# A decode step on one core: wq in plain transfers, weights of y kept in the array, and thirty-seven tiny transfers added

## The chip, the cores and the metric

The kernel runs on one core of a Trainium2 chip. A core has a matrix engine (TensorE, here PE, with its weight loads listed as PEld), a vector engine (DVE), a scalar engine (ACT), GpSimd (POOL), a sync engine (SP) that here only starts transfers, and 16 DMA engines that carry all transfers. The metric is the device time of one launch in microseconds (us), and lower is better.

## The reference

Two layers read the same normalised row and are added to the input row:

```python
x  = A_x                                  # 1 x 1 x 1024, bf16
xn = layernorm(x)
q  = (xn @ wq)                            # 32 heads of 128
k, v = last 4096 rows of the caches       # 4 kv heads, each for 8 query heads
o  = softmax(q @ k.T * 128**-0.5) @ v
A  = o.reshape(1, 1, 4096) @ wo
y  = layernorm(xn)
B  = gelu(y @ w1 + b1) @ w2 + b2          # 1024 -> 3584 -> 1024
out = x + A + B
```

One row goes in and one row comes out, so nearly all the work is reading weights and caches once: w1 and w2 of 7 MB each, wq and wo of 8 MB each, and the windows of K and V of 4 MB each.

## The kernel before, in words

The kernel is written engine by engine, with semaphores set by hand. Each engine runs its own list in order.

**Loads.** ACT starts three small loads: the row x into `XBR` (L165), b1 (L166), b2 (L167). SP starts everything large, in this order: W1 as one transfer (`load_rows`, L158), the first half of wq into `WA` (rows 0 to 3 of each partition, L158), the second half of wq in several pieces (below), two K transfers (L237), two V transfers (after the b1 products), W2 into the place of W1 (after the W1 products, semaphore count `C["h"]`), and wo into the place of wq, in pieces of 20, 10, 1 and 1 blocks (after the q products, `C["q"]`, L158). At the end it stores the row (L549).

**The second half of wq before.** Partition p holds rows 8p to 8p+7 of wq, and the second half is rows 4 to 7 of each. It is loaded in two transfers, one for the even partitions (L229) and one for the odd (L230). The odd one leaves out the last 1024 columns of row 7. These 64 pieces of 2 KB come in four transfers of 16 pieces (L233) into `WX`, a tile of 48 partitions that lies in `Pb`. Because those pieces then lie in other partitions, the product over them needs its own weights: `XPR` (x gathered by GpSimd, L183), two small products (L266), `XEZ` (L286), a copy of the weights of row 7 with the odd partitions set to zero (`EVEN`, `XNZ7`, L288 and L292), and four more products at the end of q (L354).

**Order of work.** The statistics of x and of xn (twice a short chain PE, DVE, ACT) are made while W1 is on its way. Then PE does y @ w1 (L324, 56 products, for 8 rows of `YTb` times 7 stretches of 512 columns), q (L345, 64 products, and L354), turns K (L405), scores (L431), softmax on DVE and ACT, P @ V (L510), W2 (L494) and wo (L494). Between the wo pieces stand five products of no use (L543). ACT copies the result (L547) and SP stores it.

Of the kernel before, what the change touches and what calls it, by code (L numbers as in the profile page):

```python
# [5 lines left out]
ALU = mybir.AluOpType  # L6
ACTF = mybir.ActivationFunctionType
AX = mybir.AxisListType
# [11 lines left out]
KC = D // 128  # L20
NQ = HQ * DH
WQ_CHUNKS = [4, 4]
W1_CHUNKS = [8]
W2_CHUNKS = [28]
WO_CHUNKS = [20, 10, 1, 1]
KEEP_BUSY = [[512] * 5, [], [], []]
NPAIR = HKV // 2
PB = 2 * NBLK
CUT = 1024
B1W = 256  # L30
B1N = F // B1W
XS = 2
XROWS = 48
OUTSIDE = -1e30
PAD = 32

# [13 lines left out]
def bass_parallel_sum__sliding_block_cached__mixer_channel_mlp__decode_kernel(  # L50
# [18 lines left out]
    pe, dve, act, pool, sp = nc.tensor, nc.vector, nc.scalar, nc.gpsimd, nc.sync  # L69

    def sems(name, n):
        return [nc.alloc_semaphore(f"{name}{i}") for i in range(n)]

    s_xrow, s_b1, s_b2, s_out = (nc.alloc_semaphore(n) for n in ("s_xrow", "s_b1", "s_b2", "s_out"))
    s_wq = sems("s_wq", len(WQ_CHUNKS))
    s_ex = nc.alloc_semaphore("s_ex")
    s_w1 = sems("s_w1", len(W1_CHUNKS))
    s_k = sems("s_k", NPAIR)
    s_v = sems("s_v", NPAIR)
# [4 lines left out]
    DVE = Track(nc, "S_DVE")  # L84
    ACT = Track(nc, "S_ACT")
    POOL = Track(nc, "S_POOL")

    def sb(name, shape, d):
        return nc.alloc_sbuf_tensor(name, shape, d)

    f32, bf16 = dt.float32, dt.bfloat16
    identb = sb("identb", [128, 128], bf16)
    identf = sb("identf", [128, 128], f32)
# [5 lines left out]
    oneb = sb("oneb", [128, 1], bf16)  # L99
    XBR = sb("XBR", [1, 2 * D], bf16)  # L100
    XT16 = sb("XT16", [128, 16], f32)
    msx = sb("msx", [128, 8], f32)
    XNT = sb("XNT", [128, 8], f32)
    XNTb = sb("XNTb", [128, 8], bf16)
    XNZ = sb("XNZ", [128, KC * 15], bf16)
    EVEN = sb("EVEN", [128, 1], f32)
    XNZ7 = sb("XNZ7", [128, 15], bf16)
    XPR = sb("XPR", [1, XS * XROWS], bf16)
    XEZ = sb("XEZ", [XROWS, XS * 15], bf16)
    YT16 = sb("YT16", [128, 16], f32)  # L110
    msy = sb("msy", [128, 8], f32)
    EXPW = sb("EXPW", [128, 1], f32)
# [12 lines left out]
    Pb = sb("Pb", [128, PB * HQ], bf16)  # L125
# [9 lines left out]
    W1 = sb("W1", [128, KC * F], bf16)  # L135
    W2 = W1[:, 0:FC * D]
    WA = sb("WA", [128, KC * NQ], bf16)
    WX = Pb[0:XROWS, 0:XS * CUT]
    PS = nc.alloc_psum_tensor("PS", [128, 8 * 512], f32)
    PSb = PS[:, :].bitcast(bf16)  # L140

# [1 line left out]
    b2_row = B_b2.rearrange("(o n) -> o n", o=1)  # L143
    b1_row = B_b1.rearrange("(o n) -> o n", o=1)
    wq_p = A_wq.rearrange("(p r) n -> p r n", r=KC)
    wq_runs = A_wq.rearrange("(p r) n -> p (r n)", r=KC)
    wq_x = A_wq.rearrange("(s h r e k) n -> k s h e r n", s=XS, h=2, r=4, e=4)[2 * KC - 1]
    w1_p = B_w1.rearrange("(p r) n -> p r n", r=KC)
    w2_p = B_w2.rearrange("(p c) n -> p c n", c=FC)
    wo_p = A_wo.rearrange("(p j) n -> p j n", j=32)  # L150
    out_rows = out.rearrange("b s (a n) -> (b s a) n", a=4)

    C = {}

    def load_rows(dst, src, chunks, width, semaphores):
        c0 = 0
        for j, n in enumerate(chunks):
            sp.dma_start(  # L158
                dst[:, c0 * width:(c0 + n) * width].rearrange("p (c n) -> p c n", c=n),
                src[:, c0:c0 + n, :],  # L160
            ).then_inc(semaphores[j], 16)
            c0 += n
# [3 lines left out]
    act.dma_start(B1R, b1_row.rearrange("o (c n) -> o c n", c=B1N)).then_inc(s_b1, 16)  # L166
    act.dma_start(XBR[:, D:2 * D], b2_row).then_inc(s_b2, 16)  # L167

    POOL.mark(pool.memset(WA[:, KC * NQ - CUT:KC * NQ], 0.0))
    C["hole"] = POOL.mark(pool.memset(WX, 0.0))  # L170
    POOL.mark(pool.memset(XPR[:, :], 0.0))
    C["oneb"] = POOL.mark(pool.memset(oneb[:, :], 1.0))
    C["onesf"] = POOL.mark(pool.memset(onesf[:, :], 1.0))
    POOL.mark(pool.memset(identb[:, :], 0.0))
# [1 line left out]
    C["identb"] = POOL.mark(pool.affine_select(  # L176
        out=identb[:, :], in_=identb[:, :], pattern=[[-1, 128]], compare_op=ALU.not_equal,
        fill=1.0, base=0, channel_multiplier=1))
    pool.wait_ge(s_xrow, 16)
    for i in range(XS):  # L180
        at = i * 2 * 16 * 2 * KC
        dst = XPR[0:1, i * XROWS:(i + 1) * XROWS].rearrange("o (g m) -> o g m", g=3)[:, 0:3:2, :]
        C["xpr"] = POOL.mark(pool.tensor_copy(  # L183
            dst.rearrange("o h (e r) -> o h e r", e=4),
            XBR[0:1, at + 2 * KC - 1:at + 2 * 16 * 2 * KC:2 * KC].rearrange("o (h r e) -> o h e r", h=2, e=4)))
    POOL.mark(pool.memset(identf[:, :], 0.0))
    pool.wait_ge(POOL.sem, POOL.cnt)
    C["identf"] = POOL.mark(pool.affine_select(
        out=identf[:, :], in_=identf[:, :], pattern=[[-1, 128]], compare_op=ALU.not_equal,
        fill=1.0, base=0, channel_multiplier=1))  # L190
    POOL.mark(pool.memset(XNZ[:, :], 0.0))
    POOL.mark(pool.memset(XNZ7[:, :], 0.0))
    C["xnz"] = POOL.mark(pool.memset(XEZ[:, :], 0.0))
    POOL.mark(pool.memset(E4[:, :], 0.0))
    POOL.mark(pool.memset(GMASK[:, :], 1.0))
    pool.wait_ge(POOL.sem, POOL.cnt)
# [1 line left out]
        out=E4[:, :].rearrange("p (q m) -> p q m", q=4), in_=E4[:, :].rearrange("p (q m) -> p q m", q=4),  # L198
        pattern=[[1, 4], [-1, 128]], compare_op=ALU.not_equal, fill=1.0, base=0, channel_multiplier=4))
    POOL.mark(pool.affine_select(  # L200
        out=GMASK[:, :], in_=GMASK[:, :], pattern=[[-2 * REP, NPAIR]], compare_op=ALU.is_ge, fill=0.0,
# [10 lines left out]
    at = PAR[:, :].rearrange("k (m g) -> k m g", g=2)  # L212
# [7 lines left out]
    pool.wait_ge(POOL.sem, POOL.cnt)  # L220
    POOL.mark(pool.memset(OT[:, 32:32 + PAD], 0.0))
    C["consts"] = POOL.cnt


    load_rows(W1, w1_p, W1_CHUNKS, F, s_w1)
    load_rows(WA, wq_p, WQ_CHUNKS[:-1], NQ, s_wq)
    sp.wait_ge(POOL.sem, C["hole"])
    c0 = (KC - WQ_CHUNKS[-1]) * NQ
    sp.dma_start(WA[0:128:2, c0:KC * NQ], wq_runs[0:128:2, c0:KC * NQ]).then_inc(s_wq[-1], 16)  # L229
    sp.dma_start(WA[1:128:2, c0:KC * NQ - CUT], wq_runs[1:128:2, c0:KC * NQ - CUT]).then_inc(s_wq[-1], 16)  # L230
    for i in range(XS):
        for h in range(2):
            sp.dma_start(WX[32 * h:32 * h + 16, i * CUT:(i + 1) * CUT], wq_x[i, h, :, :, NQ - CUT:NQ]).then_inc(s_ex, 16)  # L233

    def load_cache(dst, cache, semaphores):
        for i in range(NPAIR):
# [23 lines left out]
    pe.wait_ge(s_xrow, 16)  # L260
    for r in range(KC):
        last = pe.matmul(xt[:, r:r + 1], lhsT=XBR[0:1, r:D:KC], rhs=oneb[0:1, :])
    xe = PS[0:XROWS, 7 * 512 + 24: 7 * 512 + 24 + XS]
    pe.wait_ge(POOL.sem, C["xpr"])
    for i in range(XS):
        last = pe.matmul(xe[:, i:i + 1], lhsT=XPR[0:1, i * XROWS:(i + 1) * XROWS], rhs=oneb[0:1, :])  # L266
    C["xt"] = PE.mark(last)
    dve.wait_ge(PE.sem, C["xt"])
    DVE.mark(dve.tensor_copy(XT16[:, 0:8], xt))
# [12 lines left out]
    dve.wait_ge(DVE.sem, DVE.cnt)  # L282
    DVE.mark(dve.tensor_scalar(out=XNT[:, :], in0=XT16[:, 0:8], scalar1=msx[:, 2:3], scalar2=msx[:, 7:8],
                               op0=ALU.subtract, op1=ALU.mult))
    dve.wait_ge(POOL.sem, C["xnz"])
    DVE.mark(dve.tensor_scalar(out=XEZ[:, 7:XS * 15:15], in0=xe, scalar1=msx[0:XROWS, 2:3], scalar2=msx[0:XROWS, 7:8],  # L286
                               op0=ALU.subtract, op1=ALU.mult))
    C["even"] = DVE.mark(dve.tensor_reduce(out=EVEN[:, 0:1], in_=identf[:, 0:128:2], axis=AX.X, op=ALU.add))  # L288
    dve.wait_ge(DVE.sem, DVE.cnt)
    C["xn"] = DVE.mark(dve.tensor_copy(XNTb[:, :], XNT[:, :]))  # L290
    pool.wait_ge(DVE.sem, C["xn"])
    C["xnz7"] = POOL.mark(pool.tensor_tensor(out=XNZ7[:, 7:8], in0=XNTb[:, KC - 1:KC], in1=EVEN[:, 0:1], op=ALU.mult))  # L292
    dve.wait_ge(DVE.sem, DVE.cnt)
    C["xnz_d"] = DVE.mark(dve.tensor_copy(XNZ[:, 7:KC * 15:15], XNTb[:, :]))
    DVE.mark(dve.tensor_copy(YT16[:, 0:8], XNTb[:, :]))
# [7 lines left out]
    C["std2"] = ACT.mark(act.activation(out=msy[:, 6:7], in_=msy[:, 5:6], func=ACTF.Sqrt))  # L303
    act.wait_ge(ACT.sem, ACT.cnt)
    ACT.mark(act.activation(out=EXPW[:, 0:1], in_=msy[:, 6:7], func=ACTF.Exp))
    dve.wait_ge(ACT.sem, C["std2"])
    DVE.mark(dve.reciprocal(out=msy[:, 7:8], in_=msy[:, 6:7]))
    dve.wait_ge(DVE.sem, DVE.cnt)
# [10 lines left out]
    k = 0  # L319
    for j, n in enumerate(W1_CHUNKS):  # L320
        pe.wait_ge(s_w1[j], 16)
        for _ in range(n):
            for t in range(7):
                last = pe.matmul(  # L324
                    PS[0:1, t * 512:(t + 1) * 512], lhsT=YTb[:, k:k + 1],
                    rhs=W1[:, k * F + t * 512: k * F + (t + 1) * 512],
                    start=False, stop=(k == KC - 1))
            k += 1
# [6 lines left out]
    pe.wait_ge(DVE.sem, C["d_sum"])  # L335
    k = 0
    for j, n in enumerate(WQ_CHUNKS):
        pe.wait_ge(s_wq[j], 16 if j < len(WQ_CHUNKS) - 1 else 32)
        for _ in range(n):
            for t in range(8):  # L340
                cut = k == KC - 1 and (t + 1) * 512 > NQ - CUT
                if cut:
                    pe.wait_ge(POOL.sem, C["xnz7"])
                z = XNZ7[:, 7 - t:15 - t] if cut else XNZ[:, 15 * k + 7 - t:15 * k + 15 - t]
                pe.matmul(  # L345
                    PS[0:8, 7 * 512:8 * 512], lhsT=z,
                    rhs=WA[:, k * NQ + t * 512: k * NQ + (t + 1) * 512],
                    start=(k == 0 and t == 0), stop=False)
            k += 1
    pe.wait_ge(s_ex, 32 * XS)  # L350
    for i in range(XS):
        for t in range((NQ - CUT) // 512, 8):
            at = i * CUT + t * 512 - (NQ - CUT)
            last = pe.matmul(  # L354
                PS[0:8, 7 * 512:8 * 512], lhsT=XEZ[:, 15 * i + 7 - t:15 * i + 15 - t], rhs=WX[:, at:at + 512],
                start=False, stop=(i == XS - 1 and t == 7))
    C["q"] = PE.mark(last)
    dve.wait_ge(PE.sem, C["q"])
    C["d_q8"] = DVE.mark(dve.tensor_copy(Q8[:, :], PS[0:8, 7 * 512:8 * 512]))  # L359
# [183 lines left out]
            pe.matmul(PS[0:32, 0:n], lhsT=OT[:, 0:32], rhs=WA[:, 0:n])  # L543
    C["fin"] = PE.mark(last)

    act.wait_ge(PE.sem, C["fin"])
    C["a_out"] = ACT.mark(act.activation(out=ORow[:, :], in_=PS[:, 6 * 512:6 * 512 + 256], func=ACTF.Copy))  # L547
    sp.wait_ge(ACT.sem, C["a_out"])
# [32 lines left out]
```

## Time and profile before

| | |
|---|---|
| time, median of 2 runs | 100.94 us (100.84 to 101.05) |
| profiled execution, span from first to last instruction | 99.4 us |
| PE, DVE, ACT, POOL busy | 69.6, 25.8, 12.8, 9.0 us |
| bytes moved, mean rate | 39.96 MB, 402 GB/s |
| main DMA queue (SP) | 1832 packets, 39.85 MB |
| W1 products (L324) | start 20.28, 14.43 us |
| q products (L345, L354) | end 49.49 us |
| last wo products (L494) | start 95.64, 1.61 us |

The profile lists one execution. The span is counted from the first instruction to the last, and the device time of a run holds some 1.5 us more than it (100.94 against 99.4). The row of DMA digits on the page gives the mean busy share of the 16 DMA engines in 40 slices of about 2.5 us. The list of waits names for each idle stretch what ended it. Beside these views the trace holds a record of every DMA packet: its queue, start, duration and size, but not its engine. Packets that follow each other on one engine can be chained, since one starts within a few nanoseconds of the end of the other.

### The profile page before, as it was taken

How to read it: one execution, taken by the hardware profiler on the slowest of the kernel's cores; microseconds unless marked ns; L12 is line 12 of the kernel's file. 1: busy time of each engine (PE TensorE's matmuls, PEld its weight loads, DVE VectorE, ACT ScalarE, POOL GpSimd, SP SyncE). 2: the span in 40 equal slices, each digit the busy share in tenths (PEclk: the TensorE clock that was granted, in tenths of full speed). 3: DMA queues.
4: the chain of work that ended last, by engine and by line, in shares of the span. 5: the costliest groups of instructions: out<-in, count | busy, mean ns of one | idle time of the engine just before them, and what ended most of it. 6: DMA issues, size and time to landing. Idle time of an engine off the chain costs nothing.

```text
span 99.4 us, 1681 instructions
## 1 busy us (share of the span) xinstructions
PE 69.6 (70%) x763; PEld 42.4 (43%) x763; DVE 25.8 (26%) x50; ACT 12.8 (13%) x15; POOL 9.0 (9%) x30
## 2 busy tenths in 40 slices
PE   0230860089999999999999999722799995009961
PEld 0220300023434343434399869510567894008740
DVE  0058500000000090000078921867790040000000
ACT  0500240000000050000065730005200000000001
POOL 7989100000000000000000000000000000000000
PEclk9999999999999999999999999555557999855799
DMA  9988889999999999999999999998999899699930
GB/s 347 392 372 369 370 369 485 465 422 422 422 422 422 409 402 403 441 429 442 429 429 422 429 534 416 468 485 369 392 485 425 346 445 528 287 404 437 405 143 1
DMA packets 1870, 39.96 MB, mean 402 GB/s; under 512 B 244, under 2 KB 262, under 8 KB 584
## 3 DMA queue, kind: packets, MB, share of 16 engines
q1 hardware_dynamic: 1832, 39.85, 94.1%
q8 instruction: 6, 0.10, 0.4%
q10 hardware_dynamic: 32, 0.01, 0.0%
HBM read 39.86 MB, written 0.00 MB: 401 GB/s over the span
## 4 chain that ended last, share of the span: by engine, by line
DMA 65%; PE 31%; ACT 0%; SPq 0%; issue 0%
DMA WA<-in_A_wo_dram 46%; DMA W<-in_B_w_dram 19%; PE PS L324 15%; PE PS L345 14%; PE PS L494 2%; PE PS L354 1%; ACT ORow L547 0%; SPq L158 0%
## 5 line engine op out<-in xcount | busy, mean ns | idle before, releaser
L324 PE MATMUL PS<-W,YTb 128*1 128x512 bf16 x56 | 14.4, 425 | 6.2 <-DMA W<-in_B_w_dram 6.2
L345 PE MATMUL PS<-WA,XNZ 128*8 128x512 bf16 x64 | 14.0, 379 | 0.0
L324 PEld LDWEIGHTS PS<-W,YTb 128*1 128x1 bf16 x56 | 5.1, 91 | 16.0 <-issue 10.3
L510 PE MATMUL PS<-KV,Pb 128*32 128x256 bf16 x64 | 10.0, 333 | 1.2 <-ACT Pb L471 1.2
L494 PE MATMUL PS<-WA,OT 128*32 128x256 bf16 x128 | 5.6, 345 | 7.1 <-DMA WA<-in_A_wo_dram 7.1
L345 PEld LDWEIGHTS PS<-WA,XNZ 128*8 128x8 bf16 x64 | 5.6, 88 | 8.2
L510 PEld LDWEIGHTS PS<-KV,Pb 128*32 128x32 bf16 x64 | 7.4, 118 | 3.9 <-ACT Pb L471 1.7
L494 PEld LDWEIGHTS PS<-WA,OT 128*32 128x32 bf16 x128 | 4.5, 123 | 8.4 <-issue 6.3
L333 DVE CAST ROW<-PS 1x2048 bf16<-1x2048 f32 x1 | 2.3, 2279 | 22.2 <-PE PS L324 22.2
L417 ACT ACTIVATE KV<-PS 128x1024 bf16<-128x1024 bf16 x6 | 5.8, 1021 | 16.1 <-PE PS L405 16.1
L405 PE MATMUL PS<-identb,KV 128*128 128x128 bf16 x128 | 7.5, 219 | 0.0
L405 PEld LDWEIGHTS PS<-identb,KV 128*128 128x128 bf16 x128 | 7.2, 98 | 0.5 <-issue 0.4
L412 DVE COPY KV<-PS 128x1024 bf16<-128x1024 bf16 x10 | 6.4, 686 | 1.1 <-PE PS L405 1.1
L331 ACT ACTIVATE ROW<-PS 1x1536 bf16<-1x1536 f32 x1 | 1.4, 1440 | 21.2 <-PE PS L324 21.2
L359 DVE CAST Q<-PS 8x512 bf16<-8x512 f32 x1 | 0.7, 678 | 12.5 <-PE PS L354 12.5
L475 DVE TENSOR_REDUCE SUMP<-Pb 128x32 f32<-128x2048 bf16 x1 | 3.6, 3566 | 1.2 <-ACT Pb L471 1.2
L547 ACT ACTIVATE ORow<-PS 128x256 bf16<-128x256 f32 x1 | 0.4, 384 | 27.0 <-PE PS L494 27.0
L299 PE MATMUL PS<-YT,onesf 128*128 128x16 f32 x2 | 0.6, 383 | 4.2 <-DVE YT L297 4.2
L431 PEld LDWEIGHTS PS<-QT,KV 128*128 128x128 bf16 x128 | 3.3, 96 | 0.4 <-issue 0.4
L494 PE MATMUL PS<-W,GT 128*32 128x256 bf16 x112 | 3.4, 273 | 0.0
L431 PE MATMUL PS<-QT,KV 128*128 128x16 bf16 x128 | 3.4, 169 | 0.0
L442 DVE TENSOR_REDUCE MXP<-PS 128x32 f32<-128x2048 f32 x1 | 2.3, 2292 | 3.9 <-PE PS L431 3.9
(104 smaller groups left out, 48.8 us busy)
## 6 DMA issues: line engine op xcount, KB each, us to landing
W<-in_B_w_dram SPq DMA_DIRECT2D x2, 7168.0 KB, 31.0
WA<-in_A_wo_dram SPq DMA_DIRECT2D x1, 5120.0 KB, 40.0
WA<-in_A_wq_dram SPq DMA_DIRECT2D x1, 4096.0 KB, 28.6
KV<-in_A_k_cache_dram SPq DMA_DIRECT2D x2, 2048.0 KB, 40.2
KV<-in_A_v_cache_dram SPq DMA_DIRECT2D x2, 2048.0 KB, 43.6
WA<-in_A_wo_dram SPq DMA_DIRECT2D x1, 2560.0 KB, 45.7
WA<-in_A_wq_dram SPq DMA_DIRECT2D x1, 2048.0 KB, 31.2
WA<-in_A_wq_dram SPq DMA_DIRECT2D x1, 1920.0 KB, 36.7
```

The lines of the kernel that those rows point to most:

```text
L324: last = pe.matmul(PS[0:1, t * 512:(t + 1) * 512], lhsT=YTb[:, k:k + 1], rhs=W1[:, k * F + t * 512: k * F + (t + 1) * 512], start=False, s ...
L331: C["a_hrow"] = ACT.mark(act.activation(out=Hrow[:, 0:1536], in_=PS[0:1, 0:1536], func=ACTF.Copy))
L333: C["d_hrow"] = DVE.mark(dve.tensor_copy(Hrow[:, 1536:F], PS[0:1, 1536:F]))
L345: pe.matmul(PS[0:8, 7 * 512:8 * 512], lhsT=z, rhs=WA[:, k * NQ + t * 512: k * NQ + (t + 1) * 512], start=(k == 0 and t == 0), stop=False)
L405: last = pe.matmul(PSb[:, o:o + 128], lhsT=KT[:, col + bb * 128: col + (bb + 1) * 128], rhs=identb[:, :], is_transpose=True)
L412: C["dkt"][u] = DVE.mark(dve.tensor_copy(KT[:, col + 1024 * s: col + 1024 * (s + 1)], PSb[:, bk * 1024:(bk + 1) * 1024]))
L417: C["akt"][u] = ACT.mark(act.activation(out=KT[:, col + 1024: col + 2048], in_=PSb[:, bk * 1024:(bk + 1) * 1024], func=ACTF.Copy))
L431: last = pe.matmul(PS[:, o:o + 2 * REP], lhsT=KT[:, (i * PB + b) * 128:(i * PB + b + 1) * 128], rhs=QT[:, i * 2 * REP:(i + 1) * 2 * REP], ...
L442: C["mxp"] = DVE.mark(dve.tensor_reduce(out=MXP[:, :], in_=PS[:, 0:2048].rearrange("p (b n) -> p n b", b=PB), axis=AX.X, op=ALU.max))
L475: C["sump"] = DVE.mark(dve.tensor_reduce(out=SUMP[:, :], in_=Pb[:, :].rearrange("p (b n) -> p n b", b=PB), axis=AX.X, op=ALU.add))
L494: ins = pe.matmul(acc(a), lhsT=vec[:, c:c + 32], rhs=weights[:, c * D + a * 256: c * D + (a + 1) * 256], start=False, stop=(c == stop_at))
L510: last = pe.matmul(PS[0:32, 4 * 512:4 * 512 + NPAIR * DH], lhsT=Pb[:, b * HQ:(b + 1) * HQ], rhs=V4[:, :, b, :], start=(b == 0), stop=(b == ...
```

## The change

- The second half of wq becomes a plain transfer of all 128 partitions, like the first. The four transfers of `WX`, and all that served them (`XPR`, `XEZ`, `EVEN`, `XNZ7`, two large and some small fills on GpSimd (L169 to L171, L192, L193), SP's wait for these fills, six products on PE), go away.
- In y @ w1 the weights, one row of `YTb`, are loaded by the first of the seven products of a row. The other six (`again`) are issued without a weight load.
- ACT starts 15 tiny loads (`marks`) after its second table load: the n-th reads n rows of 4n bytes of x. It starts the same 15 again after the gelu's exponent, and before its last copy waits for all of them.
- GpSimd starts seven tiny loads (`PROBES`) of 2 to 7 rows, two runs of 6 to 18 bytes in each row, after its constants. ACT waits for them before the second set.

```diff
+PROBES = [3, 5, 4, 6, 7, 2, 5]
...
+    def again(out, lhsT, rhs, start, stop):
+        return pe.add_instruction(mybir.InstMatmult(
+            name=nc.get_next_instruction_name(), engine=pe.engine, ins=[pe.lower_ap(rhs), pe.lower_ap(lhsT)], outs=[pe.lower_ap(out)],
+            start_tensor_calc=start, stop_tensor_calc=stop, ldweights=False, tile_size=(128, 32), tile_position=(0, 0)))
...
+    def marks():
+        for n in range(1, 16):
+            act.dma_start(MK[0:n, n * (n - 1):n * (n + 1)],
+                          A_x.rearrange("b s (k n) -> (b s k) n", n=64)[0:n, 0:2 * n]).then_inc(s_mark, 16)
...
+    for i, n in enumerate(PROBES):
+        pool.wait_ge(s_xrow, 16)
+        pool.dma_start(
+            MP[16 * i:16 * i + n, :].rearrange("p (a n) -> p a n", a=2)[:, :, 0:i + 3],
+            A_x.rearrange("b s (k a n) -> (b s k) a n", a=2, n=32)[0:n, :, 0:i + 3]).then_inc(s_probe, 16)
...
     load_rows(W1, w1_p, W1_CHUNKS, F, s_w1)
-    load_rows(WA, wq_p, WQ_CHUNKS[:-1], NQ, s_wq)
-    sp.wait_ge(POOL.sem, C["hole"])
-    c0 = (KC - WQ_CHUNKS[-1]) * NQ
-    sp.dma_start(WA[0:128:2, c0:KC * NQ], wq_runs[0:128:2, c0:KC * NQ]).then_inc(s_wq[-1], 16)
-    sp.dma_start(WA[1:128:2, c0:KC * NQ - CUT], wq_runs[1:128:2, c0:KC * NQ - CUT]).then_inc(s_wq[-1], 16)
-    for i in range(XS):
-        for h in range(2):
-            sp.dma_start(WX[32 * h:32 * h + 16, i * CUT:(i + 1) * CUT], wq_x[i, h, :, :, NQ - CUT:NQ]).then_inc(s_ex, 16)
+    load_rows(WA, wq_p, WQ_CHUNKS, NQ, s_wq)
...
     ACT.mark(act.activation(out=EXPW[:, 0:1], in_=msy[:, 6:7], func=ACTF.Exp))
+    marks()
...
             for t in range(7):
-                last = pe.matmul(
+                put = pe.matmul if t == 0 else again
+                last = put(
                     PS[0:1, t * 512:(t + 1) * 512], lhsT=YTb[:, k:k + 1],
...
+    act.wait_ge(s_probe, 16 * len(PROBES))
+    act.wait_ge(s_mark, 16 * 15)
+    marks()
+    act.wait_ge(s_mark, 2 * 16 * 15)
     act.wait_ge(PE.sem, C["fin"])
     C["a_out"] = ACT.mark(act.activation(out=ORow[:, :], in_=PS[:, 6 * 512:6 * 512 + 256], func=ACTF.Copy))
```

More of the change, by code (lines that the diff above doesn't have):

```diff
@@ L28 @@
 PB = 2 * NBLK
-CUT = 1024
 B1W = 256
 B1N = F // B1W
-XS = 2
-XROWS = 48
 OUTSIDE = -1e30
@@ L72, in sems @@
         return [nc.alloc_semaphore(f"{name}{i}") for i in range(n)]
+    s_mark = nc.alloc_semaphore("s_mark")
+    s_probe = nc.alloc_semaphore("s_probe")
     s_xrow, s_b1, s_b2, s_out = (nc.alloc_semaphore(n) for n in ("s_xrow", "s_b1", "s_b2", "s_out"))
     s_wq = sems("s_wq", len(WQ_CHUNKS))
-    s_ex = nc.alloc_semaphore("s_ex")
     s_w1 = sems("s_w1", len(W1_CHUNKS))
@@ L104, in bass_parallel_sum__sliding_block_cached__mixer_channel_mlp__decode_kernel @@
     XNTb = sb("XNTb", [128, 8], bf16)
+    MK = sb("MK", [128, 240], bf16)
+    MP = sb("MP", [128, 20], bf16)
     XNZ = sb("XNZ", [128, KC * 15], bf16)
[L106 to L109, printed above, removed]
     YT16 = sb("YT16", [128, 16], f32)
@@ L137, in bass_parallel_sum__sliding_block_cached__mixer_channel_mlp__decode_kernel @@
     WA = sb("WA", [128, KC * NQ], bf16)
-    WX = Pb[0:XROWS, 0:XS * CUT]
     PS = nc.alloc_psum_tensor("PS", [128, 8 * 512], f32)
@@ L145, in bass_parallel_sum__sliding_block_cached__mixer_channel_mlp__decode_kernel @@
     wq_p = A_wq.rearrange("(p r) n -> p r n", r=KC)
-    wq_runs = A_wq.rearrange("(p r) n -> p (r n)", r=KC)
-    wq_x = A_wq.rearrange("(s h r e k) n -> k s h e r n", s=XS, h=2, r=4, e=4)[2 * KC - 1]
     w1_p = B_w1.rearrange("(p r) n -> p r n", r=KC)
@@ L167, in bass_parallel_sum__sliding_block_cached__mixer_channel_mlp__decode_kernel @@
     act.dma_start(XBR[:, D:2 * D], b2_row).then_inc(s_b2, 16)
-    POOL.mark(pool.memset(WA[:, KC * NQ - CUT:KC * NQ], 0.0))
-    C["hole"] = POOL.mark(pool.memset(WX, 0.0))
-    POOL.mark(pool.memset(XPR[:, :], 0.0))
     C["oneb"] = POOL.mark(pool.memset(oneb[:, :], 1.0))
@@ L178, in bass_parallel_sum__sliding_block_cached__mixer_channel_mlp__decode_kernel @@
         fill=1.0, base=0, channel_multiplier=1))
-    pool.wait_ge(s_xrow, 16)
-    for i in range(XS):
[L181 to L185, printed above, removed]
     POOL.mark(pool.memset(identf[:, :], 0.0))
@@ L190, in bass_parallel_sum__sliding_block_cached__mixer_channel_mlp__decode_kernel @@
         fill=1.0, base=0, channel_multiplier=1))
-    POOL.mark(pool.memset(XNZ[:, :], 0.0))
-    POOL.mark(pool.memset(XNZ7[:, :], 0.0))
-    C["xnz"] = POOL.mark(pool.memset(XEZ[:, :], 0.0))
+    C["xnz"] = POOL.mark(pool.memset(XNZ[:, :], 0.0))
     POOL.mark(pool.memset(E4[:, :], 0.0))
@@ L222, in bass_parallel_sum__sliding_block_cached__mixer_channel_mlp__decode_kernel @@
     C["consts"] = POOL.cnt
-    load_rows(W1, w1_p, W1_CHUNKS, F, s_w1)
-    load_rows(WA, wq_p, WQ_CHUNKS[:-1], NQ, s_wq)
-    sp.wait_ge(POOL.sem, C["hole"])
-    c0 = (KC - WQ_CHUNKS[-1]) * NQ
-    sp.dma_start(WA[0:128:2, c0:KC * NQ], wq_runs[0:128:2, c0:KC * NQ]).then_inc(s_wq[-1], 16)
-    sp.dma_start(WA[1:128:2, c0:KC * NQ - CUT], wq_runs[1:128:2, c0:KC * NQ - CUT]).then_inc(s_wq[-1], 16)
-    for i in range(XS):
-        for h in range(2):
-            sp.dma_start(WX[32 * h:32 * h + 16, i * CUT:(i + 1) * CUT], wq_x[i, h, :, :, NQ - CUT:NQ]).then_inc(s_ex, 16)
+    for i, n in enumerate(PROBES):
[3 more added lines that the diff above has]
+            A_x.rearrange("b s (k a n) -> (b s k) a n", a=2, n=32)[0:n, :, 0:i + 3]).then_inc(s_probe, 16)
+    load_rows(W1, w1_p, W1_CHUNKS, F, s_w1)
+    load_rows(WA, wq_p, WQ_CHUNKS, NQ, s_wq)
     def load_cache(dst, cache, semaphores):
@@ L262, in bass_parallel_sum__sliding_block_cached__mixer_channel_mlp__decode_kernel @@
         last = pe.matmul(xt[:, r:r + 1], lhsT=XBR[0:1, r:D:KC], rhs=oneb[0:1, :])
[L263 to L266, printed above, removed]
     C["xt"] = PE.mark(last)
@@ L284, in bass_parallel_sum__sliding_block_cached__mixer_channel_mlp__decode_kernel @@
                                op0=ALU.subtract, op1=ALU.mult))
+    dve.wait_ge(DVE.sem, DVE.cnt)
+    DVE.mark(dve.tensor_copy(XNTb[:, :], XNT[:, :]))
     dve.wait_ge(POOL.sem, C["xnz"])
[L286 to L292, printed above, removed]
     dve.wait_ge(DVE.sem, DVE.cnt)
@@ L337, in bass_parallel_sum__sliding_block_cached__mixer_channel_mlp__decode_kernel @@
     for j, n in enumerate(WQ_CHUNKS):
-        pe.wait_ge(s_wq[j], 16 if j < len(WQ_CHUNKS) - 1 else 32)
+        pe.wait_ge(s_wq[j], 16)
         for _ in range(n):
             for t in range(8):
[L341 to L346, printed above, removed]
+                last = pe.matmul(
+                    PS[0:8, 7 * 512:8 * 512], lhsT=XNZ[:, 15 * k + 7 - t:15 * k + 15 - t],
                     rhs=WA[:, k * NQ + t * 512: k * NQ + (t + 1) * 512],
-                    start=(k == 0 and t == 0), stop=False)
+                    start=(k == 0 and t == 0), stop=(k == KC - 1 and t == 7))
             k += 1
[L350 to L356, printed above, removed]
     C["q"] = PE.mark(last)
```

## The prediction

> **What bounds the kernel now.** I read the page first.
>
> ```profile
> PE 69.6 (70%) x763; PEld 42.4 (43%) x763; DVE 25.8 (26%) x50; ACT 12.8 (13%) x15; POOL 9.0 (9%) x30
> ...
> DMA  9988889999999999999999999998999899699930
> ...
> q1 hardware_dynamic: 1832, 39.85, 94.1%
> q8 instruction: 6, 0.10, 0.4%
> ```
>
> No compute engine is near full, and the DMA digits stand at 8 or 9 nearly to the end. SP's queue alone fills 94% of sixteen engines. q8 is six packets of 16 KB that belong to no line of the kernel: instruction loads. They matter below. Then the chain of waits:
>
> ```profile
> 0.81 19.34 DMA W<-in_B_w_dram
> ...
> 20.28 14.43 PE PS L324 x56
> 34.71 13.81 PE PS L345 x64
> ...
> 49.51 0.34 SPq L158
> ...
> 49.89 45.70 DMA WA<-in_A_wo_dram
> ...
> 95.64 1.61 PE PS L494 x48
> ```
>
> It goes through PE and then into wo's 45.70 us. That middle part misleads: wo waits in SP's queue behind K, V and W2, and the last W2 packet ends only at 76.9 in the packet records. So PE could issue wo some 25 us later with no effect, and the whole W1 and q stretch, the LDWEIGHTS too, has that slack. PE also idles 6.2 us before the first wo products (89.6). What sets the end is the last packet of SP's queue on the slowest of sixteen engines, 96.37 in the records. Behind it lie 3.0 us: landing, the last products, the copy, the store.
>
> How unlike the sixteen engines are is seen in one-us stretches of the end:
>
> ```profile
> 93.00:94.00 1.00, 1.00 (x25) 0.71 (x16) 0.00 (x0) 0.00 (x0) 0.00 (x0) 1.00 0.90 369
> 94.00:95.00 1.00, 0.67 (x4) 0.10 (x1) 0.00 (x0) 0.00 (x0) 0.00 (x0) 1.00 0.69 270
> 95.00:96.00 1.00, 0.36 (x16) 0.36 (x20) 0.00 (x0) 0.00 (x0) 0.00 (x0) 1.00 0.55 211
> 96.00:97.00 1.00, 1.00 (x44) 0.81 (x32) 0.00 (x0) 0.00 (x0) 0.00 (x0) 1.00 0.14 39
> ```
>
> The next to last column is the DMA share: 0.90, then 0.69, 0.55, 0.14. Some engines are done 1 to 2 us before others. Chaining the packets (each starts where the one before on its engine ended) gives seven engines that end between 94.4 and 95.1, and nine between 95.8 and 96.4. The late nine have two causes.
> Four are late from 38.5 on: the sixteen packets of each WX transfer run on only four chains, the same four each time, and these reach K 1.31 us late (38.468 to 39.777 on one).
> Five are late from an instruction load each, at 36.6, 56.2, 64.5, 75.1 and 85.9 (the sixth, 96.7, comes after the end). The first took 931 ns beside a wq packet that took 1687 instead of 1138. That engine was then 1.47 us behind. It had also been the last in W1 (19.79 against 19.26 for the first), and it is the one that ends at 96.37.
>
> **The change part by part.**
>
> *wq plain.* On every engine the second half was four packets of 32 KB and four of 30 KB; it becomes eight of 32 KB. From semaphore to semaphore the first half of wq takes 28.943 − 19.262 = 9.68 us; the second takes 38.329 − 28.943 = 9.39. So twelve engines, the five with instruction loads among them, get **+0.30 us**. The four WX engines get 0.30 − 1.31 = −1.01, but they did not set the end. SP's wait for the fills goes (2.3 us at L229); W1 and half of wq were queued by then, so nothing comes of it.
>
> *Compute of the exchange.* The XPR copies, XEZ, EVEN, XNZ7 and the long fills lie before 13.4 us, when y and the b1 products are ready, with W1 landing at 20.2: cover of 6.8 us, **0**. The four products of L354 (0.97) end q earlier; wo's issue has 25 us of cover, **0**.
>
> *Weights loaded once.* The 48 LDWEIGHTS lie under products (427 ns each while the clock is cold, then 213), and the stretch has wo's cover: **0**. With the six dropped products PE runs 60 instructions fewer. PE's are by far the longest list (1526 products and weight loads), so I take q8 to be PE's. The sixth load then probably does not occur and the fifth moves to about 90, since it falls past the wait for wo. Five still fall inside SP's stream, each costing its engine 1.47.
>
> *Tiny loads on ACT.* Issue costs ACT 0.43 to 0.85 us each (L165 to L167), 6 to 13 us a set. The first set runs from 13.6 to at most 26; ACT's next work starts at 34.75. The second starts at 70.2 and ends by 83; ACT's next work is at 97.26. Cover: 8 and 14 us. On the DMA engines they do not run for free. The small b1 load shows how:
>
> ```profile
> DMA packets 60, 1.84 MB, mean 526 GB/s; under 512 B 14, under 2 KB 28, under 8 KB 28
> ...
> q1 hardware_dynamic: 32, 1.84, 121.9%
> q10 hardware_dynamic: 28, 0.01, 0.9%
> ```
>
> This is the stretch from 6 to 9.5 us. b1's fourteen packets of 512 B and their fourteen semaphore writes stand on q10, ACT's queue. Each data packet runs between two W1 packets (6.518), and its semaphore waits until after the next W1 packet (8.654). So each tiny item gets one turn per SP packet. It costs the stream little: 24 ns of gap for 512 B, 7 for the semaphore. Fourteen rows went to fourteen chains, so I take the n-th load to go to n engines, the same low ones each time, as with WX. The first engine then gets 15 loads a set, 60 items with semaphores over both sets; a middling one gets some 24. Data of at most 60 bytes is nearer to a semaphore (4 bytes, 9 ns) than to 512 bytes: I take 8 ns an item. Below it can hardly be under 0 (no work is removed), above it is the 84 ns of a 2 KB packet. First engine 0.5 us, a middling one **+0.19**; bounds 0 and, on the first, 30 x (84 + 9) = 2.8.
>
> *Do the marks land in time?* The first engine needs 30 turns from 71.4. SP's packets left there: 2 of W2, 8 + 8 of wo's first pieces, 16 of 2 KB: 34, without their semaphores. The last mark falls between the 2 KB packets at about 95, and what is left after SP's last packet would run back to back. ACT can go on at some 96.5, before PE is done (97.2): **0**.
>
> *Tiny loads on GpSimd.* No row shows one. They start after 9 us and nothing needs them before 70. Seven loads, 64 runs and at most 16 semaphores each: some 12 items an engine, at 8 ns **+0.10**. Bounds: 0, and 12 x 84 = 1.0.
>
> On a page's word alone: the Trainium skill (DMA: Bandwidth & Descriptors, "Latency and other measured facts") says that engines 7 and 15 are usually slower, perhaps by GpSimd's descriptor rings. Before has no GpSimd transfer, so nothing here shows it, and the page gives no size.
>
> **Sum.** On the binding engine, a middling one with an instruction load: 0.30 + 0.19 + 0.10 = +0.59, so 96.37 becomes 96.96, and the span of 99.4 becomes 100.0. The time of this kernel lies 1.5 us above the span. Against the median of 100.94: **101.5 us**, or 0.6% more, well inside the 2% that a measurement of this kernel can tell from no change. Likeliest range 100.9 to 102.4.
>
> **Rivals.**
>
> A, the freed engines win: the WX engines set the end in ordinary runs, or instruction loads fall on engines that are early. For it: the WX engines end at 95.8 to 96.1, within 0.3 to 0.6 us of the last, and W1's start spreads the engines by 0.53. Against: in the trace an instruction engine is last. Price: WX engines −1.01 plus the first one's 0.5 and 0.1 gives −0.4, **100.5**; 0.18.
>
> B, tiny items are dear: 84 ns for a mark's data on the first engine, as of a 2 KB packet. It ends plainly at up to 95.1, + 0.30 + 2.8 = 98.2, 1.8 over 96.37: **102.8**. Against: b1's gap of 24 ns for more bytes. It decides once an item costs over some 30 ns, when the first engine passes the instruction engines; 0.10. The Trainium skill (DMA: Bandwidth & Descriptors, "Specifications") speaks for it: below 512 B a transfer is done as a read and a rewrite. The trace's 4-byte semaphore writes, 7 ns of gap each, show nothing of that, but they are not loads into a tile; b1's are just at the limit. The page gives no price for it.
>
> C, the marks hold the end: ACT's queue takes only a few loads at once, so that each round of three waits six turns and the 1.3 us from issue to first packet (L165 to 2.3). The turns alone last to 95; five rounds add 6.5 us of such waits, part of them in wo's long packets, and some two rounds stay after 95.5. The copy at L547 then waits about 3 us: **104**. It decides when the last mark lands after 97.2. Against: SP had twelve transfers under way by 15.3, before W1 was in; ACT had three. No row shows fifteen on ACT. 0.11.
>
> **How the numbers follow.** Forecast 0.61, A 0.18, B 0.10, C 0.11. The low end takes in A with half a us of spread (100.0), the high end B and most of what lies towards C (103.4). Slower by over 2% (above 102.96): C and a little of B, 0.13. Faster by over 2% (below 98.9) needs more than the whole lateness of the nine engines: 0.03. Within: 0.84.
>
> **What would show it.** Right: wq's second half takes 9.68 us per engine; no chain is late at 38.5 except by an instruction load; marks on q10 take about 9 ns and single turns, the first set ending at about 45; five chains 1.47 us late at the end, and the last of them ends at about 97; ACT's last copy waits for PE. Wrong: the first engine is last (B), ACT's last copy waits for a DMA (C), or the span is under 99.2 with PE's last wait shorter (A). A gain from the weights loaded once, or a longer start from GpSimd's transfers, would be outside this account.

## The result, and the profile after

The changed kernel was timed twice. Beside two runs of the kernel before it took 102.13 us against 100.94, a ratio of 1.0126 (95% interval 1.0081 to 1.0172). Beside seventeen, in six runs of its own, it took 101.35 us against 100.72: 1.0066 (1.0044 to 1.0087). Both say slower by less than 2%. The second is the narrower, and 0.63 us is next to the 0.59 of the forecast; the first, 1.19, is twice that. The profile of the first timing is the one shown here, from the page:

```profile
PE 68.0 (67%) x757; PEld 37.4 (37%) x709; DVE 25.3 (25%) x48; ACT 12.8 (13%) x15; POOL 9.7 (10%) x29
...
DMA  9888889799999999999999999988999979989810
...
q1 hardware_dynamic: 1736, 39.85, 92.9%
q8 instruction: 6, 0.10, 0.4%
q10 hardware_dynamic: 512, 0.02, 0.3%
q0 software_dynamic: 224, 0.00, 0.1%
```

PE has 54 weight loads and six products fewer, and the end comes no earlier for it. The bytes on SP's queue are the same. New are 480 tiny packets and semaphores on q10 (512 against 32) and 224 on q0, GpSimd's queue. By the page they fill 0.4% of the engines' span. The chain of waits ends as before:

```profile
49.78 47.31 DMA WA<-in_A_wo_dram
97.09 0.04 issue
97.13 1.52 PE PS L467 x48
98.65 0.02 issue
98.67 0.02 ACTq L523
98.69 0.04 issue
98.73 0.38 ACT ORow L524
```

The start of PE's last products moved from 95.64 to 97.13, and all of the 1.5 us of span lies ahead of it. ACT's wait for its tiny loads (L523, queued ahead of the wait for PE in the code) ends after PE and costs 0.02 us: the marks were in. The stretches of the end (next to last column: DMA share):

```profile
93.00:94.00 1.00, 1.00 (x27) 0.87 (x20) 0.00 (x0) 0.00 (x0) 0.00 (x0) 0.50 0.92 393
94.00:95.00 1.00, 1.00 (x26) 0.75 (x19) 0.00 (x0) 0.00 (x0) 0.00 (x0) 0.85 0.90 353
95.00:96.00 1.00, 0.87 (x5) 0.19 (x2) 0.00 (x0) 0.00 (x0) 0.00 (x0) 1.00 0.59 224
96.00:97.00 1.00, 0.00 (x0) 0.00 (x0) 0.00 (x0) 0.00 (x0) 0.00 (x0) 1.00 0.24 90
97.00:98.00 1.00, 0.87 (x32) 0.86 (x36) 0.00 (x0) 0.00 (x0) 0.00 (x0) 1.00 0.05 18
```

Two things differ from before. The bulk of the engines is later (0.90 where it was 0.69), and a single engine runs on to 97.74: 0.05 is one engine of sixteen. The packet records split the two for every kernel profiled. "Mean" is the mean end of the 256 packets of 2 KB that close SP's stream, "last" the end of the last one, in us of one profile each:

| kernel | mean | last | last − mean | ratio of times (95%) |
|---|---|---|---|---|
| before | 94.85 | 96.37 | 1.52 | 1 |
| after, first | 95.39 | 97.74 | 2.35 | 1.0126 (1.0081 to 1.0172) |
| after, again | 95.27 | 97.04 | 1.77 | 1.0066 (1.0044 to 1.0087) |
| plain wq | 94.87 | 96.98 | 2.11 | 1.0016 (0.9998 to 1.0034) |
| marks | 95.17 | 96.87 | 1.69 | 1.0063 (1.0042 to 1.0084) |
| GpSimd's loads | 94.88 | 96.27 | 1.39 | 0.9993 (0.9976 to 1.0009) |
| weights once | 95.11 | 96.80 | 1.69 | 1.0005 (0.9985 to 1.0024) |
| after without marks | 94.95 | 96.75 | 1.80 | 1.0053 (1.004 to 1.0066) |
| plain, weights once | 94.79 | 96.91 | 2.12 | 1.0027 (1.0013 to 1.0042) |
| plain, GpSimd's loads | 94.99 | 97.03 | 2.04 | 1.006 (1.0042 to 1.0079) |
| plain, low marks | 94.95 | 96.61 | 1.66 | 1.0032 (1.0015 to 1.0048) |
| plain, high marks | 95.38 | 97.00 | 1.62 | 1.0096 (1.0072 to 1.012) |

"Last" is a single draw per profile: already the first W1 packets of the sixteen engines took from 2.2 to 3.4 us each. So the mean is read from the profiles and the price from the timed runs. The mean is not clean either. The kernels without any tiny load stand at 94.79 to 95.11; the 95.11 (weights once) has no tiny packet more than before, but 16 packets of 20 KB between 88 and 92 us that took over 100 ns too long. Shifts of up to 0.3 us in one profile therefore prove little. The ratios are each to runs of the kernel before made beside them, in three groups (the four parts; the changed kernel again, without marks, and the halves of the marks; the rest). Differences between ratios of different groups are less sure than those within one.

### The profile page after: what moved, and what is told of

Read it like the earlier page. It is cut to its first block, busy times and chain, and to the rows that moved or that the text cites. A ratio compares the mean times of both kernels' runs of the same rounds, so it can differ in the third digit from the quotient of the medians.

```text
span 100.9 us, 1646 instructions
## 1 busy us (share of the span) xinstructions
PE 68.0 (67%) x757; PEld 37.4 (37%) x709; DVE 25.3 (25%) x48; ACT 12.8 (13%) x15; POOL 9.7 (10%) x29
## 4 chain that ended last, share of the span: by engine, by line
DMA 66%; PE 30%; ACT 0%; issue 0%; SPq 0%; ACTq 0%
DMA WA<-in_A_wo_dram 47%; DMA W<-in_B_w_dram 20%; PE PS L325 14%; PE PS L149 12%; PE PS L308 2%; PE PS L467 2%; ACT ORow L524 0%; SPq L163 0%; ACTq L523 0%
## 5 line engine op out<-in xcount | busy, mean ns | idle before, releaser
L149 PE MATMUL PS<-W,YTb 128*1 128x512 bf16 x48 | 14.0, 435 | 0.0
L483 PE MATMUL PS<-KV,Pb 128*32 128x256 bf16 x64 | 8.9, 311 | 1.2 <-ACT Pb L444 1.2
L308 PE MATMUL PS<-W,YTb 128*1 128x512 bf16 x8 | 3.5, 436 | 7.8 <-DMA W<-in_B_w_dram 7.8
L308 PEld LDWEIGHTS PS<-W,YTb 128*1 128x1 bf16 x8 | 0.7, 89 | 21.1 <-issue 21.1
L298 PE MATMUL PS<-KV,oneb 1*1 1x512 bf16 x7 | 3.1, 619 | 1.4 <-DMA KV<-in_B_b_dram 1.4
L218 POOL DMA_DIRECT2D MP<-in_A_x_dram x7 | 4.1, 588 | 0.1
```

The source lines that it names most:

```text
L149: return pe.add_instruction(mybir.InstMatmult(name=nc.get_next_instruction_name(), engine=pe.engine, ins=[pe.lower_ap(rhs), pe.lower_ap(lh ...
L218: pool.dma_start(MP[16 * i:16 * i + n, :].rearrange("p (a n) -> p a n", a=2)[:, :, 0:i + 3], A_x.rearrange("b s (k a n) -> (b s k) a n", a ...
L298: last = pe.matmul(PS[0:1, t * 512:(t + 1) * 512], lhsT=oneb[64:65, :], rhs=B1R[:, 2 * t:2 * t + 2, :], start=True, stop=False)
L308: last = put(PS[0:1, t * 512:(t + 1) * 512], lhsT=YTb[:, k:k + 1], rhs=W1[:, k * F + t * 512: k * F + (t + 1) * 512], start=False, stop=(k ...
L483: last = pe.matmul(PS[0:32, 4 * 512:4 * 512 + NPAIR * DH], lhsT=Pb[:, b * HQ:(b + 1) * HQ], rhs=V4[:, :, b, :], start=(b == 0), stop=(b == ...
```

## The experiments

The theory (S): the end is the slowest of sixteen DMA engines, and what counts is what lies on it. Rivals: the four engines of WX had set the end (F), a tiny transfer is dear in itself (T), GpSimd's queue has its own price (G), and moved instruction loads change the end (L).

**One part at a time, on the kernel before.** Plain wq:

```diff
-    load_rows(WA, wq_p, WQ_CHUNKS[:-1], NQ, s_wq)
-    ...
+    load_rows(WA, wq_p, WQ_CHUNKS, NQ, s_wq)
```

> The kernel before with the second half of wq in one plain transfer, and none of the tiny loads; weights loaded for every product. Theory S (the slowest DMA engine is one with an instruction load, and each term adds on it): 0.3 us longer, 101.2 us, with five engines late by 1.5 us at the end and no others. Rival F (the four engines freed of WX had set the end): 0.4 to 1.0 us shorter, 100.0 to 100.5. Rival T (all of the 1.2 us comes from tiny transfers): no change, 100.9.

Measured: 1.0016 (0.9998 to 1.0034), +0.16 us; F, a gain, is out. S's 0.3 us and T's nothing both lie within the interval. In the packet records each half of wq takes 9.68 us on every engine (semaphores from 19.469, 29.150 and 38.831), so twelve engines did get 0.30 us. At K only one engine was late, the one with an instruction load, where before five were. The mean end did not move (94.87): twelve times +0.30 less four times 1.01 is almost nothing. At the end of the profile five chains are late (96.3 to 97.0, the other eleven by 95.2), as theory S had it, where before nine were. The stretch from 95 to 96 shows it in the DMA share, 0.27 where before had 0.55:

```profile
95.00:96.00 1.00, 1.00 (x5) 0.30 (x3) 0.00 (x0) 0.00 (x0) 0.00 (x0) 0.73 0.27 100
96.00:97.00 1.00, 0.95 (x30) 0.69 (x32) 0.00 (x0) 0.00 (x0) 0.00 (x0) 1.00 0.18 70
```

So the late engines became fewer and, in this profile, later.

The marks:

```diff
+    marks()                                   # after EXPW, 15 loads
...
+    act.wait_ge(s_mark, 16 * 15)
+    marks()
+    act.wait_ge(s_mark, 2 * 16 * 15)
     act.wait_ge(PE.sem, C["fin"])
```

> The kernel before with both sets of ACT's tiny loads and the waits for them, and nothing else. Theory S: a middling engine gets some 30 items of 7 to 12 ns, 0.2 to 0.4 us longer, 101.1 to 101.3. Rival T (tiny items are dear, or the copy waits for them): 0.9 us longer or more, 101.8. Rival N (they ride along): no change, 100.9.

Measured: 1.0063 (1.0042 to 1.0084), +0.63 us, between S and T. The two sets are 240 loads' packets and as many semaphores, 30 items an engine. The mean end is 0.32 us later, which would be 11 ns an item if all of it were theirs; the kernel with the weights once, below, moves by 0.26 with no item added. The records give the price of a turn directly: where a tiny packet runs between two large ones, the second starts 5 to 8 ns later than without it.

GpSimd's loads and the wait for them (`PROBES`, as in the change):

> The kernel before with GpSimd's seven tiny loads and the wait for them, and nothing else. Theory S: 12 to 14 items an engine of 6 to 12 ns, 0.1 us longer, 101.0. Rival G (a GpSimd queue has a cost of its own at the start or the end of a launch): 0.5 us longer or more, 101.5.

Measured: 0.9993 (0.9976 to 1.0009). G is out: no cost of a GpSimd queue at the start or the end of this launch is seen. S's own 0.1 us lies just above the interval (at most 0.09).

The weights once per row:

```diff
-                last = pe.matmul(
+                put = pe.matmul if t == 0 else again
+                last = put(
```

> The kernel before with the weights of y loaded once per row of W1, and nothing else. Theory S: five instruction loads as before, each on its own engine, 100.9 and no change. Rival L (48 instructions fewer move the instruction loads to engines that are late anyway, or drop one): 0.3 to 1.0 us longer or shorter, 101.5 or 100.2.

Measured: 1.0005 (0.9985 to 1.0024). The first instruction load moved from 36.6 to 43.7, as a shorter PE list would have it, with no effect here.

**The sum of parts, and where marks lie.** The changed kernel again:

> The changed kernel again, beside more runs of the kernel before. If the parts add (plain wq 0.16, marks 0.63, GpSimd's loads -0.07, weights loaded once 0.05 us): 0.8 us longer than before, ratio 1.008. If they do something together that none does alone: 1.2 us, ratio 1.012.

Measured: 1.0066 (1.0044 to 1.0087). The parts' sum, 0.77 us, lies within; the 1.2 us of the first timing does not.

Without both sets of marks:

> The changed kernel without both sets of ACT's tiny loads. If the parts add: 0.15 us longer than before, ratio 1.0015, and ACT's loads are most of the change. If plain wq, GpSimd's loads and the instruction order work together: ratio 1.004 to 1.006.

Measured: 1.0053 (1.004 to 1.0066), more than the parts' 0.15 us. So the marks, 0.63 us alone, add only some 0.13 on top of the other three, and the other three are worth more together than apart. The parts do not add, although their plain sum comes near.

Plain wq with half of the marks: n from 1 to 7 (engines 0 to 6 alone) or from 8 to 15, each load twice a set.

```diff
-        for n in range(1, 16):
+        for at in (0, 56):
+            for n in range(1, 8):             # the other: (-56, 128) and range(8, 16)
...
+                act.dma_start(MK[0:n, at + n * (n - 1):at + n * (n + 1)],
```

> Plain wq as in the kernel with that alone (ratio 1.0016 to before), and of ACT's tiny loads only those of 1 to 7 rows, each twice a set: 28 loads, on engines 0 to 6 alone. Theory S with instruction loads on engines 7 to 11 (as the tiny loads' sizes mark them in the trace of after): the engines that end last get nothing, no change to plain wq, ratio 1.0016. Rival T (a tiny load has a price wherever it runs, on ACT or in the wait): as much as the other half, 0.5 us, ratio 1.006 or 1.007.

> The same with the tiny loads of 8 to 15 rows, each twice a set: 32 loads. Engine 7 gets 64 items, engine 11 gets 32. Theory S at 9 ns an item: 0.3 to 0.6 us over plain wq, ratio 1.005 to 1.0075. Rival T: the same as with the loads of 1 to 7 rows. Should the marks of the second set land after the last products, ACT's copy waits for a DMA and the ratio is over 1.01.

Measured: low 1.0032 (1.0015 to 1.0048), high 1.0096 (1.0072 to 1.012). These lines of the two pages give the packets, low first:

```profile
q1 hardware_dynamic: 1736, 39.85, 93.9%
q8 instruction: 6, 0.10, 0.4%
q10 hardware_dynamic: 256, 0.01, 0.2%
```

```profile
q1 hardware_dynamic: 1736, 39.85, 93.5%
q10 hardware_dynamic: 768, 0.03, 0.5%
q8 instruction: 6, 0.10, 0.4%
```

The low half is 56 loads in both sets and costs 0.16 us over plain wq; the high half is 64 and costs 0.8. A price per transfer, T, is out: it goes by packets. Less the 32 of the three first loads, q10 has 224 and 736 packets and semaphores, 14 and 46 an engine; the mean end moves by 0.08 and 0.51 us (some 0.1 of the latter is packets of 20 KB that took too long). That the low ones cost less because their engines are not the last ones is not shown by this, since they are also fewer. High, the last mark is in at 96.3 and ACT's copy waits for PE.

The sizes of the marks name the engine (engine 0 carries n = 1 to 15, engine 5 carries n = 6 to 15), and they correct the place that I had given to the instruction loads. In the changed kernel (first profile) an engine whose first packets of the second set are those of n = 6 or n = 7 runs in the same chain as the first or the second instruction load, n = 10 as the third, n = 11 ahead of the fourth and n = 12 behind it: engines 5, 6, 9 and 10, read with care, since some packets are missing in the records. The second profile has the same. In the kernel before with marks the fourth load runs ahead of a lone n = 15 and the fifth between n = 9 and n = 10 of a chain that begins with n = 6: engines 14 and 5. So they do not all lie on engines 7 to 11, as my expectations say, and they are not the same in all kernels.

The marks also name the engine that ends last. In both profiles of the changed kernel, and in the kernel before with marks, the last 20 KB packet is in the chain with n = 6 to 15, engine 5, and an instruction load is in that chain as well, as far as the records let it be followed. Engine 5 carries 40 items. In the first profile it can be followed from 97.74 back to the packet behind the first instruction load, save for a gap of 0.13 us at 80.8; with that gap, three of its steps after 77 us are longer than their like, by 0.08, 0.13 and 0.27 us. That is half of the 0.9 us by which it ends behind the next engine.

**An attempt at a better kernel.** If the last engines are known, load can be taken off them. On plain wq:

```diff
-    load_rows(WA, wo_p, WO_CHUNKS, D, s_wo)
+    load_rows(WA, wo_p, WO_CHUNKS[:-1], D, s_wo)
+    for p0, p1 in ((0, 119), (119, 128)):     # the control: 112
+        sp.dma_start(WA[p0:p1, 31 * D:32 * D], wo_p[p0:p1, 31, :]).then_inc(s_wo[-1], 16)
```

> Plain wq as in the kernel with that alone (ratio 1.0016), and the last block of wo, 2 KB in each of 128 partitions, in two transfers: partitions 0 to 118 and 119 to 127. 119 rows are 7 times 17, so the first runs on engines 0 to 6, 17 packets each, and the second, of 9 rows, on engines 0 to 8. Engines 7 and up are relieved of 0.57 to 0.65 us, engines 0 to 6 get 0.8 us, of which they have 1.4 to spare. Theory S (the end is set by engines from 7 up, those with an instruction load): 0.4 to 0.6 us shorter than plain wq, ratio to before 0.996 to 0.998. Rival E (the engines are alike, or those that end last are other ones): seven engines get 0.8 us more, ratio 1.008 to 1.010.

> As the first of these, with the cut of the last block at partition 112: 112 rows and 16 rows, both over all sixteen engines. As many transfers, and all engines alike. Theory S and rival E both: no change to plain wq, ratio 1.002. If cutting the transfer, and not where it runs, is what matters, it goes as the other cut does.

Measured: 1.0141 (1.0092 to 1.019), and the control 1.0102 (1.0083 to 1.0122). Both are worse than plain wq. The intervals overlap, and the six runs of the unbalanced one fall into two groups: three at 101.6 us and three at 102.7 to 103.0. The control's six lie from 101.6 to 102.0. The profile is of one of the three long runs. From its end, in stretches:

```profile
96.00:97.00 1.00, 0.32 (x8) 0.13 (x10) 0.00 (x0) 0.00 (x0) 0.00 (x0) 1.00 0.22 76
97.00:98.00 1.00, 1.00 (x44) 0.97 (x36) 0.00 (x0) 0.00 (x0) 0.00 (x0) 1.00 0.13 51
98.00:99.00 1.00, 0.29 (x16) 0.03 (x4) 0.00 (x0) 0.00 (x0) 0.00 (x0) 1.00 0.08 23
```

From 97 on, 0.13 of the engines is two of sixteen: two chains, late already with their last 20 KB packet (96.2, the other at about 95.7), run 2 KB packets back to back until 98.32 and 98.05. The last holds 26 of them, so it is one of the engines that got seventeen more. It can be followed back, through three packets of 20 KB that took 0.16, 0.16 and 0.40 us too long, to the packet behind the third instruction load (63.1). So in this run an instruction load lay on an engine below 7, as the marks show in other kernels, and the idea fell with the place of the loads. What made the other three runs shorter no trace shows.
The control shows a second thing: cutting the last block, with all engines alike, costs 0.86% over plain wq, which was timed in another group. In its records some forty of the 2 KB packets from 94.7 to 96 take 125 to 165 ns instead of 84, and late packets of 20 KB up to 1251 instead of 764. Why is open.

**What lifts the kernel without marks.**

> Plain wq and the weights of y loaded once, without any tiny load. Weights loaded once on top of before gave 1.0005, plain wq 1.0016, both with GpSimd's loads 1.0053. If the later instruction loads (43, 61, 69, 82 and 94 us in the trace of the kernel without ACT's loads) cost something once the four low engines are free: 1.004 to 1.005. If not: 1.002.

> Plain wq and GpSimd's seven tiny loads, without ACT's and with weights loaded for every product. Theory S: 12 to 14 items an engine of 6 to 12 ns over plain wq, 0.1 us, ratio 1.0025. If GpSimd's loads are what lifts the kernel without ACT's loads to 1.0053: 1.004 to 1.005.

Measured: with the weights once 1.0027 (1.0013 to 1.0042), with GpSimd's loads 1.006 (1.0042 to 1.0079). So it is mostly GpSimd's loads, which cost nothing on the kernel before and 0.44% on plain wq (by ratios of two groups). The first of the two kernels also shows that an instruction load makes an engine late. With plain wq alone the load came at 36.7, and one engine reached K at 40.62 while the others did by 39.5. With the weights once it came at 43.7; all sixteen reached K by 39.41, and the late one appears after the second K transfer, at 50.13 against 49.13 for the next.

No kernel tried beats the one before.

## Why the prediction was right or wrong

**The bound: right.** SP's stream on the slowest engine set the end, and the terms on PE were nothing: L354's products gone, 54 weight loads fewer, wo issued at 49.40 instead of 49.51, and no gain. The kernel with the weights once alone shows it for the weight loads (1.0005); L354 went with the wq change and was not timed alone. The late engines are those with an instruction load, as the forecast had it: in the profile of before the five last chains without WX packets each lead back to one of the five loads.

**wq, +0.30 us on twelve engines: right as a row, not settled as a term.** Per engine it is 9.68 us where it was 9.39. In the time it is 0.16 (at most 0.34), so 0.30 is not excluded. If it is too large, the step would be that I added it to the last engine as if it were fixed. Before, nine engines shared the last place; with plain wq five do, and the slowest of five draws of a start that spreads by half a us is lower than the slowest of nine. This reading fits, and is not tested.

**Marks, +0.19 us: too small on the kernel before.** Alone they are worth 0.63 there (0.42 to 0.85). The mechanism held: single turns, nothing late at ACT, first set over by 45. The turn was priced about right, 5 to 8 ns for the 8 assumed. The count was wrong: I charged "a middling engine" 24 items, when sixteen engines carry 30 on average and the one that ended last carried 40. That gives 0.2 to 0.3 us. The rest of the 0.63 is not shown: some large packets took 100 to 270 ns too long, but such packets stand in profiles without tiny loads too. On top of the other three parts the marks cost some 0.13, with intervals that overlap, which is near the term.

**GpSimd's loads, +0.10: near on the kernel before (−0.07, at most +0.09), too small on plain wq (+0.44).** Their 224 packets are 14 an engine, not 12: one for each of the 32 rows with both its runs, 112 semaphore writes, and 80 of 8 bytes that I had not counted. At 5 to 8 ns they should be 0.1 us. The other 0.3 us is open. Which engines get the instruction loads differs between kernels, so two kernels can differ by a draw of that kind; no run here took this apart.

**The sum, +0.59: near, and partly by luck.** Measured 0.63 in the second timing and 1.19 in the first, both within the likeliest range. The terms as timed alone (0.16, 0.63, −0.07, 0.05) are not those that I added up, and the changed kernel without marks is already 0.53 longer. So the total came out although the marks' term is a third of what they cost alone. That a load on an engine that is not last is free would make the parts together less than their sum; 0.63 against 0.77 is within the noise and does not show it.

**Rivals.** A (a gain from the freed engines) fell with plain wq at no gain. B fell by size: the marks' packets of 8 to 60 bytes took 8 to 11 ns in the records, and the first engine was not the last. The Trainium skill (DMA: Bandwidth & Descriptors, "Specifications") has transfers below 512 B done as a read and a rewrite; no price of that is seen here. C (marks hold ACT) fell: 0.02 us at L523, and the queue took fifteen loads without a stop: 4.33 us for ten, 0.43 each.

**Instruction loads.** Five inside SP's stream, one engine late for each, right in number and price: the packets behind them took 1158 instead of 611, 2609 instead of 2116, 2022 instead of 1514. Their places were less sure. The forecast had the fifth at about 90 and no sixth. In the first profile of the changed kernel the fifth came at 86.3 and a sixth at 98.3, after SP's stream; in the second the fifth came at 94.3 and no sixth is listed.

## What to carry to other kernels

When transfers fill all DMA engines to the end, count what each engine carries and not only the bytes: the end is the slowest engine, and the mean share on the profile's page hides a spread of two us. A small transfer that rides along such a stream took a turn of 5 to 8 ns here for each packet and each semaphore on the engine that carries it. Count them on the engine that is last, not on a middling one. Timed, the thirty tiny loads cost more than these turns on one kernel and less on another, so a price from one kernel does not carry over unmeasured. An edit that lightens only engines that are not last buys nothing (the WX engines, freed of 1.01 us each), and one meant to lighten the last must first show which those are, in that very kernel.

## What the runs showed of the hardware that I had not expected

- An instruction load of 16 KB (q8) holds one DMA engine for about 1.5 us: 0.9 to 1.1 us of its own, and 0.5 us that the packet behind it takes longer. The 16 KB of a data packet take 0.61. The Trainium skill (Runtime: NRT & Kernel Launch, "Instruction fetch mechanics") calls the cost of a new 16 KB block mostly hidden; the lists of waits put none of PE's down to one, but the DMA engines do lose the time.
- The engine that it lands on is not the same in all kernels: 5, 6, 9 and 10 for the first four in the changed kernel, 14 and 5 for the fourth and fifth in the kernel before with marks, as far as the marks tell.
- A data packet and its own semaphore each wait for a turn, one large packet apart: 2.1 us beside 57 KB packets. The first set of marks, begun at 9.4 us, was all in only by 45.
- In the kernel with the weights once 16 of the 75 packets of 20 KB that start between 88 and 92 us took over 100 ns longer than 764, the longest 1248. The unbalanced kernel has 16 as well, the control 10, the one with high marks 8, before none. What it is stays open.
